# Attention rounds woven into an FFN and expert kernel: normalising written ahead of the transposition, and the weight split of three double rounds written behind their softmax

## The chip, the cores and the metric

One core of a Trainium2 chip runs the whole program in one launch. The metric is the device time of that launch in microseconds (us). Shown for the kernel before are the median of three runs and one execution that was also profiled.

## What is computed

The reference, cut to what matters:

```python
# attention: B 2, H 8, S 768, D 64, n_global 8, n_local 96
scores = q @ k^T / sqrt(D) + bias          # bias: -slope * distance
scores = where(keep, scores, -1e9)         # keep: global keys or a local window
a = exp(scores - max(scores)); a = a / (sum(a) + 1e-9)
x = (a @ v), tokens x 512                  # 1536 tokens
# feed-forward (wff), 512 -> 2048 -> 512
h = x @ w_in; g = h * tanh(softplus(h)); y = g @ w_out
# experts (wts), 4 of 512 -> 1024 -> 512, all tokens through all experts
out = sum over e of p[:, e] * (relu(y @ w1[e]) @ w2[e])
```

All of it is float32. The kernel gets float32 accuracy out of a faster matmul type by splitting each factor into a high part (a cast, `...h`) and a low part (the difference, `...l`), and multiplying high by high, low by high and high by low.

## The kernel before

**Blocks and steps.** The 1536 tokens are three blocks of 512. Block 0 goes through attention and the feed-forward part first (`first_block`, ordered by the string `PLAN`). Then `run` walks over steps `s`: each step is one chunk of hidden columns. Steps 16 to 46 are chunks of the experts for block 0. While they run, the attention of blocks 1 and 2 is woven in: 32 pairs (a tile of 128 queries by two heads), each of which goes through the stages of `Attention`. Then come the feed-forward steps of blocks 1 and 2, and the experts of these two blocks (`late_block`).

**A step with attention.** TensorE does the twelve products of the hidden chunk (`hidden`, line 648), the scores of a pair (lines 265 and 266, tile `s`), the transposition of the pair before (line 205, tile `pt`, four 128x128 pieces, head 0 and head 1 in turn), the twelve products of `project` (line 737, tile `acc`) and the product of the transposed probabilities with the values (line 312, tile `o`).

**The stages of a pair in round r** (`Attention`): `scores(r)`; `softmax(r)`, which first gathers an older output (`of`, lines 329 and 332, `x..h` and `x..l`, lines 333 and 334), then on VectorE adds the bias and finds the row extreme (line 279, tile `t`), and on ScalarE takes the exponential with its row sums (line 290, tile `p`); `norm(r)`, two small VectorE instructions on the row sums (lines 192 and 193, tile `st`) and then the scaling of `p` by two instructions of GpSimd (line 200), or of ScalarE (line 198) for the first three pairs; `trans(r-1)`, the transposition of the pair before and its split (high on ScalarE, line 302; low on VectorE, line 303); `parts`, which splits the q and k of a coming pair (lines 239, 241, 244, 246) and the v of this one (lines 254 and 255); `av(r-2)` with the copies of line 320. A pair is transposed one round after its scores.

**Weights.** `part(s)` splits the weights of a coming step: a high part on ScalarE (`wh`, line 630) and a low part in two instructions on GpSimd (`wl`, line 633). It is called for two steps ahead (`now("part", min(s + 3, last))`).

**Double rounds.** 31 steps don't hold 35 rounds, so steps 27, 35 and 43 (`EXTRA = 11, 19, 27` behind step 16) make two: the first one's scores and softmax stand ahead of `hidden`, its other stages behind it, and the second round follows with the usual places. Below, A is the pair whose softmax is in the first half of such a step, and B the one in its second half; B is transposed in the step behind it (28, 36 and 44).

**What sets the order.** Nothing is rescheduled: each engine executes its instructions in the order in which the Python code issues them, and waits on semaphores where data or a buffer is not ready. The order of the calls in `run` is thus the order on every engine's queue.

Of the kernel before, what the change touches and what calls it, by code (L numbers as in the profile page):

```python
# [543 lines left out]
class Body:  # L544
# [420 lines left out]
    def flush(self):  # L965
        for run in self.later:
            run()
        self.later = []
# [35 lines left out]
    def late_block(self, project):  # L1004
# [22 lines left out]
        for run in held[:2]:  # L1027
            run()
# [9 lines left out]
        for run in held[2:]:  # L1038
            run()
# [170 lines left out]
    def run(self):  # L1210
        tc = self.tc
        ffn = lambda t: [("ffn", t, f) for f in range(NF1)]
        moe = lambda a, b: [("moe", 0, f) for f in range(a, b)]

        cut = NE * NF2 - 1
        steps = ffn(0) + moe(0, cut) + ffn(1) + ffn(2) + moe(cut, NE * NF2)
        last = len(steps)
        self.steps = steps
        self.opens, self.closes = set(), {}
        for s, (kind, t, n) in enumerate(steps):  # L1220
            per = NF1 if kind == "ffn" else NF2
            if n % per == 0 or s == last - 1:
                self.opens.add(s)
            if n % per == per - 1 or n == cut - 1:
                self.closes[s] = 0 if n == NF2 - 1 and kind == "moe" else 1 if s == last - 1 else 2
        self.x, self.y, self.outs, self.nr, self.yf, self.rows = {}, {}, {}, {}, {}, {}
        self.w64, self.w32, self.ws, self.h, self.enr, self.g = {}, {}, {}, {}, {}, {}
        self.seconds = {}
        self.w2, self.wp, self.late, self.held = {}, {}, None, None
        bias = self.bias.rearrange("p h c -> p (h c)")  # L1230
        self.sums, self.rest = [bias[:, 0:1024], bias[:, 1024:2048]], bias[:, 2048:3072]
        ready = dict(fetch=0, narrow=0, part=0)

        def now(what, upto):
            while ready[what] < min(upto, last):
                for _ in getattr(self, what)(ready[what]) or ():
                    pass
                ready[what] += 1

        need = [steps.index(("ffn", t, 0)) for t in range(1, NB)]  # L1240
        ffn_at = lambda s: 0 <= s < last and steps[s][0] == "ffn"
        if self.first:
            att, done = self.first_block(ready, now)
            s0 = NF1
        else:
            att, done, s0 = Attention(self, self.pair, 0), 0, 0
            while att.round():
                pass
            att, self.accumulating = None, True
            self.probabilities()  # L1250
        for s in range(s0, last):
            if s == NF1 and not att:
                att = Attention(self, self.pair, 1, NB - 1)
            if s == need[1]:
                while att and att.round():
                    pass
                att = None
                self.attending.close()
                self.late = self.ctx.enter_context(tc.tile_pool(name="late", bufs=1))
            if self.wide and s < NF1:  # L1260
                while ready["narrow"] < min(s + 3, NF1):
                    now("fetch", ready["narrow"] + 1)
                    now("narrow", ready["narrow"] + 1)
            if ffn_at(s - 1) and done < s:
                self.mish_newton(s - 1)
            if s == NF1 and done < s:

                self.mish_hi(s - 1)
                self.mish_lo(s - 1)
                self.project(s - 2)  # L1270
                self.project(s - 1)
                done = s
            now("part", min(s + 3, last))
            if att:
                att.ahead()
            rest, att = (att, None) if s == need[0] - 2 else (None, att)
            extra = att and s - NF1 in EXTRA
            if extra:
                att.scores()
                att.softmax()  # L1280
            self.hidden(s)
            if extra:
                att.trans()
                att.norm()
                att.parts()
                att.av()
                att.ahead()
            if att:
                att.scores()
            if ffn_at(s):  # L1290
                self.mish_exp(s)
            else:
                self.relu_hi(s)
            if att:
                att.softmax()
            if not ffn_at(s):
                self.relu_lo(s)
            if ffn_at(s - 1) and done < s:
                self.mish_hi(s - 1)
            if ffn_at(s):  # L1300
                self.mish_cap(s)
                self.mish_n(s)
                self.mish_r(s)

                if ffn_at(s - 1):
                    self.mish_lo(s - 1)
            if not self.wide or ready["narrow"] == NF1:
                now("fetch", s + 6)
            follow = bool(s0) and s == NF1 + 1
            if follow:  # L1310
                self.project(done)
                done += 1
            if att and not extra:
                att.trans()
                att.norm()
                att.parts()
            if ffn_at(s - 1) and not ffn_at(s) and done < s:
                self.mish_lo(s - 1)
            if not follow and done <= s - (1 if s0 and att and s < need[0] - 2 else 2):
                self.project(done)  # L1320
                done += 1
            if extra:
                att.trans()
                att.norm()
                att.parts()
            if att and not att.av():
                att = None
            att = att or rest
            for task in {8: (("weights", 0, "in"), ("weights", 1, "in")), 6: (("sums", 0),), 5: (("sums", 1),),
                         3: (("part", 0, "in"), ("weights", 0, "out")), 2: (("part", 0, "sums"),),  # L1330
                         1: (("part", 1, "in"),)}.get(last - s, ()):
                getattr(self, "late_" + task[0])(*task[1:])
        self.late_start()
        self.late_part(0, "out")
        self.late_block(lambda k: self.project(last - 2 + k))
# [61 lines left out]
```

## Time and profile before

| | |
|---|---|
| median of 3 runs | 882.5 us (881.11 to 882.75) |
| the profiled execution | 882.74 us, of it 880.9 us span from the first to the last instruction |
| TensorE busy | 865.2 us, 98% of the span |
| VectorE, ScalarE, GpSimd busy | 575.1, 495.1 and 407.5 us (65%, 56%, 46%) |
| mean granted TensorE clock | 0.997 of full speed |
| chain that ended last | TensorE 80%, VectorE 9%, DMA 4%, issue 2%, ScalarE 2%, GpSimd 1% |

A busy engine is one whose instructions overlap that time; the records of matmuls overlap each other, so a matmul's recorded length is longer than the distance from its start to the next start. A row of the timeline gives start, length, engine, line, tile and operands, and in square brackets the idle time just ahead of the instruction and what ended it by the profile's inference. The attention of blocks 1 and 2 lies between about 141 and 357 us.

### The profile page before, as it was taken

Reading aid. Unit: us, or ns where it says so; the run is one execution under the profiler, and the core shown is the slowest. Engines: PE = TensorE matmul, PEld = TensorE weight load, DVE = VectorE, ACT = ScalarE, POOL = GpSimd, SP = SyncE. Lnnn points to the kernel's source line nnn. Section 1 sums busy time; section 2 is a strip of 40 time slices with the busy share of each in tenths; the row PEclk is TensorE's granted clock in tenths of the full one; section 3 lists DMA queues with packets and bytes.
Section 4 is the critical chain, followed back from the end, with each engine's and each line's share of the span. In section 5 each row is a group of like instructions: output and inputs, shape, how many; then the busy total and the mean of one; then the engine's idle time right before and its main releaser. Section 6 shows DMA issues by size and latency. Waiting matters only on the chain.

```text
span 880.9 us, 11412 instructions
## 1 busy us (share of the span) xinstructions
PE 865.2 (98%) x3892; PEld 677.8 (77%) x3892; DVE 575.1 (65%) x1108; ACT 495.1 (56%) x971; POOL 407.5 (46%) x431
## 2 busy tenths in 40 slices
PE   8899998999999999999999999999999999999997
PEld 4545656888888888888888888788888888888886
DVE  6999996766777775566656667645555555555555
ACT  6667576878877777577675567533333333333330
POOL 4001333777776877555310225554455555544420
PEclk9999999999999999999999999999999999999999
DMA  8479782444444442888555640511111111111002
GB/s 316 171 247 282 263 310 96 162 171 145 168 144 145 167 168 73 307 290 289 223 194 198 241 167 1 186 54 48 48 48 48 49 57 62 49 48 48 1 1 99
DMA packets 40579, 127.47 MB, mean 145 GB/s; under 512 B 4160, under 2 KB 6976, under 8 KB 38464
## 3 DMA queue, kind: packets, MB, share of 16 engines
q1 hardware_dynamic: 39648, 125.32, 40.6%
q0 software_dynamic: 720, 1.31, 0.8%
q8 instruction: 32, 0.52, 0.2%
q14 instruction: 35, 0.29, 0.1%
q10 hardware_dynamic: 144, 0.02, 0.0%
HBM read 97.02 MB, written 28.31 MB: 142 GB/s over the span
## 4 chain that ended last, share of the span: by engine, by line
PE 80%; DVE 9%; DMA 4%; issue 2%; ACT 2%; POOL 1%; SPq 0%; DVEq 0%; ACTq 0%; POOLq 0%
PE acc_l L985 20%; PE acc L737 19%; PE h L648 18%; PE ha L934 9%; PE hx L934 7%; DMA wfirst<-w 2%; PE pt L205 2%; DVE w L612 2%; PE o L312 1%; DVE w L614 1%; DMA qk<-in_qk 1%; DVE w L610 1%; PE acc L821 1%; DVE nr L688 1%; PE s L266 1%
## 5 line engine op out<-in xcount | busy, mean ns | idle before, releaser
L633 POOL TENSOR_TENSOR wl<-w,wh 128x512 fp32r<-128x512 f32 x94 | 123.6, 1335 | 67.5 <-ACT wh L630 54.3
L838 DVE SCALAR_TENSOR_TENSOR big<-acc_l,prob,big 128x512 f32<-128x512 f32 x120 | 88.8, 746 | 78.9 <-PE acc_l L985 78.7
L917 POOL TENSOR_TENSOR zl<-wout,zh 128x512 fp32r<-128x512 f32 x32 | 40.9, 1303 | 85.2 <-ACT zh L915 85.2
L917 POOL TENSOR_TENSOR sumsl<-bias,sumsh 128x512 fp32r<-128x512 f32 x32 | 42.7, 1355 | 69.3 <-ACT sumsh L915 69.3
L947 ACT COPY raw<-ha 128x512 f32<-128x512 f32 x33 | 19.4, 586 | 79.6 <-PE ha L934 79.6
L684 DVE SCALAR_TENSOR_TENSOR nr<-e,n 128x512 f32<-128x512 f32 x48 | 34.1, 711 | 44.1 <-ACT n L679 43.8
L664 ACT ACTIVATE e<-h 128x512 f32<-128x512 f32 x48 | 28.1, 586 | 60.8 <-PE h L648 25.5
L200 POOL TENSOR_SCALAR p<-p,st 128x256 f32<-128x256 f32 (+1 forms) x58 | 41.5, 726 | 36.6 <-ACT v L254 31.9
L648 PE MATMUL h<-y0h,wh 128*128 128x512 f32 x128 | 51.0, 398 | 2.1 <-ACT y0h L754 1.9
L737 PE MATMUL acc<-wh,gh 128*128 128x512 f32 x128 | 52.4, 409 | 0.0
L648 PE MATMUL h<-y0l,wh 128*128 128x512 f32 x128 | 51.0, 398 | 0.7 <-DVE y0l L755 0.7
L648 PE MATMUL h<-y0h,wl 128*128 128x512 f32 x128 | 50.9, 398 | 0.0
L985 PE MATMUL acc_l<-zh,gh 128*128 128x512 f32 x128 | 50.7, 396 | 0.0
L985 PE MATMUL acc_l<-zh,gl 128*128 128x512 f32 x128 | 50.5, 394 | 0.0
L630 ACT CAST wh<-w 128x1024 fp32r<-128x1024 f32 x48 | 50.1, 1045 | 0.7
L985 PE MATMUL acc_l<-zl,gh 128*128 128x512 f32 x128 | 50.4, 394 | 0.0
L737 PE MATMUL acc<-wh,gl 128*128 128x512 f32 x128 | 50.2, 392 | 0.0
L985 PE MATMUL acc_l<-zh,gl_late 128*128 128x512 f32 (+1 forms) x128 | 50.0, 391 | 0.0
L985 PE MATMUL acc_l<-zh,gh_late 128*128 128x512 f32 (+1 forms) x128 | 50.0, 391 | 0.0
L737 PE MATMUL acc<-wl,gh 128*128 128x512 f32 x128 | 50.0, 390 | 0.0
L737 PE MATMUL acc<-gh,wh 128*128 128x512 f32 x128 | 49.8, 389 | 0.0
L737 PE MATMUL acc<-gh,wl 128*128 128x512 f32 x128 | 49.8, 389 | 0.0
(254 smaller groups left out, 2521.3 us busy)
## 6 DMA issues: line engine op xcount, KB each, us to landing
w<-in_wts SPq DMA_DIRECT2D x32, 512.0 KB, 4.6
raw<-in_qkv SPq DMA_DIRECT2D x32, 512.0 KB, 3.6
big<-in_wff SPq DMA_DIRECT2D x10, 1024.0 KB, 6.4
wfirst<-w SPq DMA_DIRECT2D x16, 512.0 KB, 11.0
w<-wfirst SPq DMA_DIRECT2D x16, 512.0 KB, 4.7
wkeep<-wh SPq DMA_DIRECT2D x16, 512.0 KB, 4.0
wkeep<-wl SPq DMA_DIRECT2D x16, 512.0 KB, 3.0
wh<-wkeep SPq DMA_DIRECT2D x16, 512.0 KB, 3.2
```

Of the source, the lines that this page charges most:

```text
L200: nc.gpsimd.tensor_scalar(p, p, r, 0.0, ALU.mult, ALU.add)
L630: (nc.vector.tensor_copy if copy == "vector" else nc.scalar.copy)(hi, w)
L633: getattr(nc, engine or "gpsimd").tensor_tensor(lo[:, c], w[:, c], hi.bitcast(F32)[:, c], ALU.subtract)
L648: nc.tensor.matmul(ps, a[:, c], r[:, kc, :], start=m == 0, stop=m == 3 * KC - 1)
L664: nc.scalar.activation(e, self.h[s], AF.Exp, scale=0.5)
L684: nc.vector.scalar_tensor_tensor(self.nr[s], e, 1.0, n, ALU.add, ALU.mult)
L737: nc.tensor.matmul(acc[:, h], a, r, start=opens and k == 0 and m == 0, stop=closes and k == len(chunks) - 1 and m == 2)
L838: nc.vector.scalar_tensor_tensor(o, acc, p, o, ALU.mult, ALU.add)
L917: nc.gpsimd.tensor_tensor(lo[:, c], w[:, c], hi.bitcast(F32)[:, c], ALU.subtract)
L934: nc.tensor.matmul(ps, a[:, c], r[:, kc, :], start=opens and n == 0, stop=n == 5, skip_group_check=True)
L947: nc.scalar.copy(t[(1, 6, 7).index(m)], ps)
L985: nc.tensor.matmul(o, a[:, c], r[:, w], start=n == 0, stop=n == 5)
```

## The change

Two things, both in the order of calls in `run`. In every round there the call of `norm` is written ahead of `trans` (it was behind). And in the three double steps `part` is no longer called at the start of the step: it is called behind the softmax of the second round and the `relu_lo`.

```diff
-            now("part", min(s + 3, last))
             if att:
                 att.ahead()
             rest, att = (att, None) if s == need[0] - 2 else (None, att)
             extra = att and s - NF1 in EXTRA
-            if extra:
+            if not extra:
+                now("part", min(s + 3, last))
+            else:
                 att.scores()
                 att.softmax()
             self.hidden(s)
             if extra:
+                att.norm()
                 att.trans()
-                att.norm()
                 att.parts()
                 att.av()
                 att.ahead()
...
             if not ffn_at(s):
                 self.relu_lo(s)
+            if extra:
+                now("part", min(s + 3, last))
             if ffn_at(s - 1) and done < s:
                 self.mish_hi(s - 1)
...
             if att and not extra:
+                att.norm()
                 att.trans()
-                att.norm()
                 att.parts()
...
             if extra:
+                att.norm()
                 att.trans()
-                att.norm()
                 att.parts()
```

No computing instruction is added, taken away or resized on any engine; the orders of TensorE and of the DMA queue (SP) stay as they were. Where the other three differ:

GpSimd in the double step 35, before (`x2l` is the low part of a gathered output, `wl` that of the weights, `p_1` is pair A, `p_2` pair B):

```order
L334 TENSOR_TENSOR x2l<-of_2_2903,x2h 128x128
L200 TENSOR_SCALAR p_1_2910<-p_1_2910,st_1_2912 128x256 x2
L255 TENSOR_TENSOR v_1_2949<-raw_122,v_1_2949 128x2x128
L334 TENSOR_TENSOR x2l<-of_3_2967,x2h 128x128
L200 TENSOR_SCALAR p_2_2974<-p_2_2974,st_2_2976 128x256 x2
L255 TENSOR_TENSOR v_2_3016<-raw_123,v_2_3016 128x2x128
```

and in the change:

```order
L334 TENSOR_TENSOR x2l<-of_2_2898,x2h 128x128
L200 TENSOR_SCALAR p_1_2905<-p_1_2905,st_1_2907 128x256 x2
L255 TENSOR_TENSOR v_1_2944<-raw_122,v_1_2944 128x2x128
L334 TENSOR_TENSOR x2l<-of_3_2962,x2h 128x128
L633 TENSOR_TENSOR wl_2979<-w_2669,wh_2978 128x512 x2
L200 TENSOR_SCALAR p_2_2969<-p_2_2969,st_2_2971 128x256 x2
```

The two `wl` instructions stood ahead of the first row before; now they stand directly ahead of the scaling of pair B. Steps 27 and 43 differ in the same way.

ScalarE in the second half of the same step, in the change (`gh` is the high part of the hidden chunk, `p_2` with `st_2` the exponential of pair B, `pt_1` the transposed pair A):

```order
L712 ACTIVATE gh_2960<-h_2912 128x512
L333 CAST x2h<-of_3_2962 128x128
L290 ACTIVATE p_2_2969,st_2_2971<-t_2_2970,st_2_2971 128x256 x2
L630 CAST wh_2978<-w_2669 128x1024
L302 CAST pt_1_3006<-pt_1_3001 128x4x128
L239 CAST qs_0_3009<-raw_122 128x256
```

Before, `L630 wh` stood ahead of the gather of the first half, and `L302` followed `L290` directly.

VectorE in the second half of the same step, before:

```order
L717 SCALAR_TENSOR_TENSOR gl_2981<-h_2917,gh_2965 128x512
L303 TENSOR_TENSOR pt_1_3002<-pt_1_2997,pt_1_3002 128x4x128
L192 TENSOR_SCALAR st_2_2976<-st_2_2976 128x2
L193 RECIPROCAL st_2_2976<-st_2_2976 128x2
L244 TENSOR_TENSOR qs_0_3009<-raw_122,qs_0_3009 64x256
```

and in the change:

```order
L717 SCALAR_TENSOR_TENSOR gl_2976<-h_2912,gh_2960 128x512
L192 TENSOR_SCALAR st_2_2971<-st_2_2971 128x2
L193 RECIPROCAL st_2_2971<-st_2_2971 128x2
L303 TENSOR_TENSOR pt_1_3006<-pt_1_3001,pt_1_3006 128x4x128
L244 TENSOR_TENSOR qs_0_3009<-raw_122,qs_0_3009 64x256
```

The two small instructions on the row sums (`st`) moved ahead of the low part of the transposed pair (`pt`); this is so in every one of the rounds from step 16 on.

## Rows read from the trace of the kernel before

**Rows 1.** The page's busy time by engine, over the whole span:

```profile
PE 865.2 (98%) x3892; PEld 677.8 (77%) x3892; DVE 575.1 (65%) x1108; ACT 495.1 (56%) x971; POOL 407.5 (46%) x431
```

**Rows 2.** The waits of PE: us in total, times, longest:

```profile
PE h L648 <- ACT y0h L754: 1.9, 1, 1.9
...
PE pt L205 <- POOL p L200: 1.1, 3, 0.4
```

**Rows 3.** Busy time by stretch, between two double steps:

```profile
231.00:280.00 49.00, 49.00 (x260) 41.81 (x259) 36.31 (x108) 37.18 (x97) 38.57 (x45) 1.00 0.47 161
```

**Rows 4.** PE in order of time: transpositions in steps 19, 28, 36 and 44:

```profile
167.04 0.27 PE L205 MATMUL pt<-ident,p 128*128 128x128 f32 x1
167.57 0.55 PE L205 MATMUL pt<-ident,p 128*128 128x128 f32 x3 [0.26 <-POOL p L200]
...
230.27 0.55 PE L205 MATMUL pt<-ident,p 128*128 128x128 f32 x3 [0.41 <-POOL p L200]
...
287.53 0.27 PE L205 MATMUL pt<-ident,p 128*128 128x128 f32 x1
288.22 0.55 PE L205 MATMUL pt<-ident,p 128*128 128x128 f32 x3 [0.42 <-POOL p L200]
...
344.37 0.60 PE L205 MATMUL pt<-ident,p 128*128 128x128 f32 x4
```

**Rows 5.** POOL in order of time, step 18, ahead of the first wait:

```profile
165.14 0.46 POOL L334 TENSOR_TENSOR x1l<-of,x1h 128x128 fp32r<-128x128 f32 x1
166.01 1.51 POOL L200 TENSOR_SCALAR p<-p,st 128x256 f32<-128x256 f32 x2 [0.41 <-ACT v L254]
```

**Rows 6.** POOL in order of time, double step 35:

```profile
277.42 2.52 POOL L633 TENSOR_TENSOR wl<-w,wh 128x512 fp32r<-128x512 f32 x2
...
283.76 0.46 POOL L334 TENSOR_TENSOR x2l<-of,x2h 128x128 fp32r<-128x128 f32 x1 [0.52 <-ACT x2h L333]
286.65 1.51 POOL L200 TENSOR_SCALAR p<-p,st 128x256 f32<-128x256 f32 x2 [2.42 <-ACT v L254]
```

**Rows 7.** ACT in order of time, double step 35:

```profile
276.20 1.05 ACT L630 CAST wh<-w 128x1024 fp32r<-128x1024 f32 x1
...
284.82 0.19 ACT L290 ACTIVATION_READ_ACCUMULATOR p<-t,st 128x1 f32 x1
284.91 0.57 ACT L302 CAST pt<-pt 128x512 fp32r<-128x512 f32 x1
```

**Rows 8.** DVE in order of time, double step 35:

```profile
279.88 0.69 DVE L303 TENSOR_TENSOR pt<-pt,pt 128x512 fp32r<-128x512 f32 x1 [1.52 <-ACT pt L302]
280.49 0.16 DVE L192 TENSOR_SCALAR st<-st 128x2 f32<-128x2 f32 x1
...
280.88 0.42 DVE L244 TENSOR_TENSOR qs<-raw,qs 64x256 fp32r<-64x256 f32 x1
281.33 0.85 DVE L246 TENSOR_TENSOR kl<-raw,kh 128x512 fp32r<-128x512 f32 x1
...
286.31 0.17 DVE L193 RECIPROCAL st<-st 128x2 f32<-128x2 f32 x1
```

**Rows 9.** ACT and POOL in the double steps 27 and 43:

```profile
226.97 0.57 ACT L302 CAST pt<-pt 128x512 fp32r<-128x512 f32 x1
...
341.54 0.56 ACT L302 CAST pt<-pt 128x512 fp32r<-128x512 f32 x1
...
343.27 0.93 POOL L200 TENSOR_SCALAR p<-p,st 128x256 f32<-128x256 f32 x2 [2.27 <-DVE st L193]
```

**Rows 10.** DVE and POOL where both split a k at once, and DVE alone:

```profile
142.38 1.48 POOL L246 TENSOR_TENSOR kl<-raw,kh 128x512 fp32r<-128x512 f32 x1
...
142.83 1.58 DVE L246 TENSOR_TENSOR kl<-raw,kh 128x512 fp32r<-128x512 f32 x1
...
154.61 0.69 DVE L246 TENSOR_TENSOR kl<-raw,kh 128x512 fp32r<-128x512 f32 x1
```

**Rows 11.** Busy time by stretch where the clock was lower; PEclk is third from last:

```profile
145.00:149.00 4.00, 3.93 (x10) 3.11 (x11) 1.81 (x4) 0.04 (x1) 1.25 (x2) 0.57 0.71 260
```

## The prediction

> **What bounds the kernel now.** I read the busy time by engine first, then TensorE's waits, then its timeline where a wait is, then the other engines at those places. TensorE is busy 98% of the span [rows 1], and between two double steps it is busy without a gap, 49.00 of 49.00 us, while the other three have over ten us of slack [rows 3]. So in an ordinary round nothing that VectorE, ScalarE or GpSimd do earlier is worth anything, and the change can act only where TensorE waits for the chain that it reorders. TensorE waits for GpSimd's scaling of `p` three times [rows 2]: at transpositions in step 19, and in steps 28 and 36, each just behind a double step [rows 4]. Idle time understates such a loss, since records overlap; I take it from starts. The second piece of a transposition follows the first by 0.09 us where nothing is waited for (four pieces then take 0.35). In step 36 it came 288.22 - 287.53 = 0.69 behind the first, so 0.60 was lost there, and in step 19 0.53 - 0.09 = 0.44. In step 44 there was no wait [rows 4].
>
> **Who releases the scaling.** The page names ScalarE's `v` as releaser of GpSimd's `p`, but `p` doesn't read `v`. The reciprocal of pair B ended at 286.31 + 0.17 = 286.48 and `p` started at 286.65 [rows 6, 8]; in step 43 the same start is put down to the reciprocal [rows 9]. So the true chain is: row sums, `st`, `p`, transposition. The sums were there at 284.82 + 0.19 = 285.01 [rows 7], and `st` waited 1.3 us longer only because it was queued behind the low part of the transposed pair.
>
> **Part 1, normalising ahead.** In every round `st` can now start at the row sums, and takes 280.88 - 280.49 = 0.39 us [rows 8] in the gap in which VectorE sits waiting for ScalarE's copy (1.52 us ahead of `L303` in step 35). So `L303` is not later, and whatever follows on VectorE is up to 0.39 earlier. GpSimd's `p` could start about 1 us earlier. In ordinary rounds TensorE covers that: worth nothing [rows 3]. In the first three pairs it is ScalarE that scales, now ahead of its copy of `pt`; that copy comes later, but the product that needs it stands a whole projection behind. In step 18 the gain is limited by GpSimd's queue: it is busy with `x1l` until 165.14 + 0.46 = 165.60, and `p` started at 166.01 [rows 5], so the transposition of step 19 gains 0.41 (0 to 0.44). One wait is written out that was implied: a transposition reuses the bank of the one before, so it needs that one's `L303`, which `st` no longer guarantees. At the worst place, step 36, `L303` ends near 286.7 by the working below, before the first piece at 287.53.
>
> **Part 2, the weight split behind the second softmax.** Nothing is saved where it stood: ScalarE and GpSimd had idle time there. What counts is what now queues behind it. On ScalarE `wh` (1.05) stands ahead of pair A's copy `L302`, the q, k and v copies and the copies of the output; on GpSimd `wl` (2.52) stands directly ahead of pair B's scaling [rows 6, 7], and B is the pair that TensorE asks for in the next step. In step 35, in the times of the old trace:
> - `L302` started at 284.91 [rows 7]. VectorE's chain into B's exponential is 0.39 earlier, so `wh` starts at 284.52 and ends at 285.57. GpSimd has been idle since `x2l`, ended at 284.22 [rows 6], and starts `wl` some 0.1 later, at 285.67; it ends at 288.19.
> - Then `p`. It took 1.51 us in step 35 and 0.93 in step 43 [rows 6, 9]; the difference is VectorE's split of q and k, which runs over the one and is absent by the other. In the new order `L302` ends near 286.1, `L303` takes 0.61 behind it, and the split 0.45 + 0.85 [rows 8], from 286.7 to 288.0: it lies over `wl` instead, so I take 0.93, and `wl` becomes dearer by what a GpSimd subtraction lost in such an overlap, 1.48 against 2.52 / 2 = 1.26 [rows 6, 10]: 0.2. `p` ends at 289.32, and TensorE goes on 0.06 later (288.16 to 288.22 in rows 4 and 6), at 289.38 in place of 288.22: **+1.2** (+1.0 without the overlap, +1.75 with the slow `p` as well).
>
> I take VectorE's lead as 0.3 in the other two, since there ScalarE's copies of line 320 hold part of it back.
> - Step 27: `L302` at 226.97 [rows 9]; wh from 226.67, `wl` 227.82 to 230.54, `p` to 231.47, TensorE at 231.53 in place of 230.27 [rows 4]: **+1.25** (+1.0 to +1.75).
> - Step 43: `L302` at 341.54 [rows 9]; `wh` to 342.29, `wl` 342.39 to 344.91, `p` (0.93, no q or k to split any more) to 345.84, TensorE at 345.90. It needed that piece at 344.37 + 0.09 = 344.46: **+1.45** (+1.25 to +1.75).
>
> At places like these the Trainium skill has a rule that speaks against the change, in SBUF — State Buffer, Who interferes with whom: a VectorE instruction with two SBUF inputs and a GpSimd instruction that reads SBUF don't share, the one that starts later is blocked for the whole of the other. The trace agrees for most of it: VectorE's split of k took 0.69 alone, 0.85 under `p`, and 1.58 under GpSimd's own split, which itself lost only 0.2 [rows 8, 10]. By the rule in full, a `wl` caught behind both splits would lose 0.42 + 0.69 = 1.1 in place of 0.2, at two of the places.
>
> Other effects I cost at nothing. The weights split later are used in the step after next, with the whole of step 36 between. Their `w` buffer comes free some 8 us later, and the load that takes it is for four steps on. VectorE and ScalarE fall behind by about 1 us in step 36, which is no more than TensorE has lost there. Behind the attention TensorE is bound by its own work, so nothing given away is recovered.
>
> **Sum.** -0.41 + 1.25 + 1.2 + 1.45 = +3.5 us; each place is counted against its own old resume, so they add. Bounds: -0.44 + 1.0 + 1.0 + 1.25 = +2.8, and 0 + 3 x 1.75 = +5.3. The profiled execution took 882.74, which would become 886.2; it stands 0.24 above the median of 882.5, from which I forecast **886.0**.
>
> **Rivals.**
> - *The stalls go (faster).* If the new split were done before TensorE asks for B, the reordered `st` would remove the losses: 0.41 and two of 0.60, and at most VectorE's lead of 0.3 at each of the two, if TensorE also waits there for a bank that VectorE frees: -2.2, 880.3. This needs `wh`, `wl` and `p` to fit between 284.5 and 287.6, 3.1 us, where the rows give 1.05 + 2.52 + 0.93 = 4.5. It decides at a `wl` of some 1.1 us, under half of its row. 6%.
> - *They cancel (no difference).* If the two places that had a wait resume where they did, and only step 43's is new: -0.41 + 1.45 = +1.0, 883.5. For it: the chain would have to be shorter by 1.2 at both, as by softmaxes earlier than I reckon. 12%.
> - *The clock falls.* After its longest wait in the middle of the program, 1.9 us for `y0h` [rows 2], TensorE ran from 145 to 149 us with a granted clock of 0.57 on the mean, mostly at the lower of 1.2 and 2.4 GHz [rows 11], which cost 0.43 x 4.00 = 1.7 us. The new waits are of up to about that size (0.6 + 1.25 in step 28). Against it: the old wait in step 28 left the clock at 1.00 [rows 3, 4], and a transposition breaks each new one in two. One fall makes 887.7, two 889.4. 10%.
> - *Full blocking.* `wl` waits out both of VectorE's splits, 0.42 + 0.69 = 1.1 in place of 0.2 [rows 8, 10], as VectorE lost 0.9 to GpSimd where the two split a k at once: 0.9 more at two places, +5.3, 887.8. 6%. This is the rule of the Trainium skill given above.
>
> **The numbers.** The forecast as such has 66%, with its bounds 885.3 to 887.8. With half of the no-difference case and the single fall of the clock, the range is 884.3 to 888.2. About 0.2% (1.8 us) is what a measurement of this kernel can tell from no change. Slower: 66 + 10 + 6 = 82%; the same 12%; faster 6%.
>
> **What would show it.** Right: in the double steps GpSimd's two `wl` end just ahead of B's `p`; TensorE waits for `p` in steps 28, 36 and 44, at the first piece already, and no longer in step 19; `p` takes about 0.93 there; the clock stays at 1.00. Wrong: no wait in step 44; `p` of pair B starting ahead of 288; a wait in ordinary rounds; or a stretch of lower clock behind one of the three.

## The result and the profile after

The change makes the kernel slower: 889.95 us median of six executions (887.54 to 891.44) against 881.81 (880.78 to 882.75) before, a ratio of 1.009 with a 95% interval of 1.0074 to 1.0105. The forecast of 886.0 had the direction, but its range ended at 888.2. The profiled execution of after took 890.03, of it 888.2 us span; that of before took 882.74, as its table says.

The page of after, busy time by engine:

```profile
PE 867.2 (98%) x3892; PEld 679.2 (76%) x3892; DVE 590.7 (66%) x1108; ACT 495.1 (56%) x971; POOL 400.8 (45%) x431
```

Beside [rows 1] two things moved that no edit explains at first sight: VectorE is busy 15.6 us longer with the same 1108 instructions, and GpSimd 6.7 us less. The waits of PE, after:

```profile
PE pt L205 <- POOL p L200: 5.3, 3, 2.0
...
PE o L312 <- DVE of L332: 0.7, 1, 0.7
```

Three waits for `p` of 1.1 us in all [rows 2] became three of 5.3, and there is a wait for VectorE that was not there. The timeline of PE, after, at the places of [rows 4] and at the new wait in step 35:

```profile
166.80 0.60 PE L205 MATMUL pt<-ident,p 128*128 128x128 f32 x4
...
230.93 1.36 PE L205 MATMUL pt<-ident,p 128*128 128x128 f32 x4 [1.99 <-POOL p L200]
...
286.57 0.71 PE L312 MATMUL o<-pt,v 128*128 128x256 f32 x4 [0.65 <-DVE of L332]
...
292.75 1.00 PE L205 MATMUL pt<-ident,p 128*128 128x128 f32 x4 [1.97 <-POOL p L200]
...
350.92 0.89 PE L205 MATMUL pt<-ident,p 128*128 128x128 f32 x3 [1.37 <-POOL p L200]
```

In step 19 the four pieces run together again (x4 in one row), as before the change they did not. In steps 28, 36 and 44 the first piece waits.

To see what each place cost I pair the n-th matmul of after with the n-th of before (their order is the same) and follow how the distance of their starts grows. From 160 us on it changes at six places: step 19 -0.42; steps 27 and 28 +1.81; between 231 and 235 us, with no wait, +1.44; step 35 +0.55; step 36 +1.90; step 44 +1.93. The sum is +7.2, which is the difference of the profiled executions (7.3). The third of these is no wait at all. Busy time by stretch, after (the number of matmuls stands in brackets behind PE's busy time, PEclk third from last):

```profile
145.00:149.00 4.00, 4.00 (x13) 3.19 (x14) 1.61 (x3) 0.20 (x1) 1.06 (x1) 0.60 0.76 271
231.00:235.00 4.00, 3.90 (x12) 3.10 (x13) 3.60 (x11) 3.00 (x9) 4.00 (x6) 0.57 0.43 140
235.00:284.00 49.00, 49.00 (x260) 41.80 (x260) 38.97 (x103) 34.21 (x90) 31.64 (x43) 1.00 0.42 150
```

Behind the wait of 1.99 us in step 28 the granted clock was 0.57 on the mean, so mostly at the lower of its two levels (1.2 and 2.4 GHz), and TensorE began 12 matmuls in four microseconds, where at the higher clock it begins 260 in 49, so 21 in four. That is +1.44. It is the same sight as [rows 11], which after has too. The last line answers to [rows 3]: between the double steps TensorE is still without a gap.

The spread goes with these falls. The six executions of after fall into pairs by mean granted clock: 887.54 and 888.49 at 0.997, 889.88 and 890.03 at 0.995, 891.05 and 891.44 at 0.993. The profiled one, at 0.995, has two falls (145 us and 231 us), and the profiled one of before, at 0.997, has one. At the same mean clock of 0.997, so with one fall each, after is 5 to 6 us slower (887.54 and 888.49 against executions of before at 882.1 to 882.6); the rest of the 8.1 us between the medians I put down to the clock.

What TensorE waited for in step 36 was made in step 35. Here is that step after the change: ACT in order of time (with the `wh` of steps 27 and 43), then POOL (with the `p` of step 27 and the `wl` and `p` of step 43), then DVE:

```profile
226.16 1.03 ACT L630 CAST wh<-w 128x1024 fp32r<-128x1024 f32 x1
...
286.46 0.30 ACT L333 CAST x2h<-of 128x128 fp32r<-128x128 f32 x1 [1.38 <-DVE of L332]
...
287.98 1.04 ACT L630 CAST wh<-w 128x1024 fp32r<-128x1024 f32 x1
...
346.76 1.03 ACT L630 CAST wh<-w 128x1024 fp32r<-128x1024 f32 x1
```

```profile
229.96 1.37 POOL L200 TENSOR_SCALAR p<-p,st 128x256 f32<-128x256 f32 x2
...
283.97 0.75 POOL L255 TENSOR_TENSOR v<-raw,v 128x256 fp32r<-128x256 f32 x1 [0.17 <-ACT v L254]
286.83 0.46 POOL L334 TENSOR_TENSOR x2l<-of,x2h 128x128 fp32r<-128x128 f32 x1 [2.12 <-ACT x2h L333]
289.10 2.71 POOL L633 TENSOR_TENSOR wl<-w,wh 128x512 fp32r<-128x512 f32 x2 [1.80 <-ACT wh L630]
291.78 1.38 POOL L200 TENSOR_SCALAR p<-p,st 128x256 f32<-128x256 f32 x2
...
347.86 2.54 POOL L633 TENSOR_TENSOR wl<-w,wh 128x512 fp32r<-128x512 f32 x2 [1.79 <-ACT wh L630]
350.38 0.94 POOL L200 TENSOR_SCALAR p<-p,st 128x256 f32<-128x256 f32 x2
```

```profile
284.09 1.17 DVE L246 TENSOR_TENSOR kl<-raw,kh 128x512 fp32r<-128x512 f32 x1
...
288.31 0.17 DVE L193 RECIPROCAL st<-st 128x2 f32<-128x2 f32 x1
...
290.70 1.65 DVE L246 TENSOR_TENSOR kl<-raw,kh 128x512 fp32r<-128x512 f32 x1
```

Read the chain backwards: TensorE (292.75) waits for B's `p` (from 291.78), that stands behind `wl` (from 289.10), and `wl` for `wh` (from 287.98), for which GpSimd stood idle for 1.80 us. The reciprocal that `p` reads was done at 288.48, 3.3 us before `p` began. VectorE's `kl` began at 290.70, under the second `wl` instruction, and ended 0.54 after `wl` did; in that time `p` made little way, and took 1.38 where in step 43, without a `kl`, it took 0.94.

### The profile page after: what moved, and what is told of

The parts are those of the page before. It is cut to its first block, busy times and chain, and to the rows that moved or that the text cites. A ratio compares the mean times of both kernels' runs of the same rounds, so it can differ in the third digit from the quotient of the medians.

```text
span 888.2 us, 11437 instructions
## 1 busy us (share of the span) xinstructions
PE 867.2 (98%) x3892; PEld 679.2 (76%) x3892; DVE 590.7 (66%) x1108; ACT 495.1 (56%) x971; POOL 400.8 (45%) x431
## 4 chain that ended last, share of the span: by engine, by line
PE 79%; DVE 9%; DMA 3%; issue 3%; ACT 2%; POOL 2%; SPq 0%; DVEq 0%; POOLq 0%; ACTq 0%
PE acc_l L985 20%; PE acc L737 18%; PE h L648 18%; PE ha L934 9%; PE hx L934 7%; DMA wfirst<-w 2%; PE pt L205 2%; DVE w L612 1%; PE o L312 1%; DVE w L614 1%; DMA qk<-in_qk 1%; DVE w L610 1%; PE acc L821 1%; DVE nr L688 1%; ACT p L290 1%
## 5 line engine op out<-in xcount | busy, mean ns | idle before, releaser
L630 ACT CAST wh<-w 128x1024 fp32r<-128x1024 f32 x48 | 50.0, 1045 | 0.6
L737 PE MATMUL acc<-gl,wh 128*128 128x512 f32 x128 | 49.8, 389 | 0.0
```

What stands on the lines that cost most here:

```text
L630: (nc.vector.tensor_copy if copy == "vector" else nc.scalar.copy)(hi, w)
L737: nc.tensor.matmul(acc[:, h], a, r, start=opens and k == 0 and m == 0, stop=closes and k == len(chunks) - 1 and m == 2)
```

## Experiments

Three theories were in play. **1:** the loss is GpSimd's queue: the split of the weights stands ahead of B's scaling. **2:** it is norm ahead, whose early `p` runs over VectorE's split of q and k. **3:** it is `wh` on ScalarE, ahead of A's copy and all that follows there.

### Norm ahead alone (e1_norm_only)

The kernel before, with part 1 of the change and without part 2:

```diff
-                att.trans()
                 att.norm()
+                att.trans()
                 att.parts()
```

in all three places.

> The first part of the change alone: norm ahead of trans in every round, the weight split of the double steps at their start as before. Theory 1 (the loss is the queue on GpSimd, the weight split standing ahead of pair B's scaling): no wait in steps 28, 36 and 44, none in step 19; -0.4 - 0.6 - 0.6 = -1.6 us, up to 0.5 given back in step 35 where TensorE now waits for a bank: between -1.9 and -0.9. Theory 2 (the earlier scaling runs over VectorE's split of q and k, and that slowdown is the loss): slower than before by 1 us or more. Theory 3 (the weights' high part standing ahead of pair A's copy on ScalarE is the loss): as theory 1 here. All: the split of k on VectorE takes about 1.17 us in ordinary rounds in place of 0.85.

Measured: 880.86 us median (879.29 to 882.83) against 882.17 of the kernel before on the same chip, ratio 0.9991 (0.9982 to 1.0001). PE in order of time in this kernel, steps 27, 28 and 36:

```profile
225.09 0.47 PE L312 MATMUL o<-pt,v 128*128 128x256 f32 x2 [0.32 <-DVE of L332]
...
229.13 0.60 PE L205 MATMUL pt<-ident,p 128*128 128x128 f32 x4
...
286.25 0.60 PE L205 MATMUL pt<-ident,p 128*128 128x128 f32 x4
```

No wait for `p` is left: step 19 gained 0.43, step 28 0.57, step 36 0.58, and step 35 0.19; step 27 lost 0.42 to a wait for VectorE. Something to be given back was expected, but in step 35. In step 27 it was the `st` of pair A, on VectorE:

```profile
221.07 0.69 DVE L192 TENSOR_SCALAR st<-st 128x2 f32<-128x2 f32 x1 [0.88 <-ACT p L290]
```

Written early, it began while GpSimd was at the step's own `wl`, and took 0.69 in place of 0.16 [rows 8]: it ended at 221.76, `wl` at 221.74. VectorE's split of k took 1.16 on the median, as expected (1.17). So theory 2 can't be the loss of 8 us. The gain is there in the trace; the ratio's interval just includes 1.

### The split moved alone (e2_split_only)

The change, with `norm` behind `trans` again in all three places:

```diff
-                att.norm()
                 att.trans()
+                att.norm()
                 att.parts()
```

> The second part of the change alone: the weight split of the double steps behind the second softmax, norm behind trans as before. Theory 1: waits for the scaling in steps 28, 36 and 44 as long as in the change, +1.5 to +2.0 us each, no gain in step 19: +4.5 to +6.0, and 1.7 more for each fall of the clock. Theory 2: within 1 us of before. Theory 3: as theory 1. VectorE's split of k stays at 0.85 in ordinary rounds.

Measured: 889.91 (889.64 to 890.23), ratio 1.0094 (1.0079 to 1.0109). Places: steps 28 and 36 +1.9 each, step 44 +1.75, and a fall of the clock behind step 36, +1.6. Part 2 alone is the loss. PE, POOL and DVE of this kernel, step 36:

```profile
290.89 0.33 PE L205 MATMUL pt<-ident,p 128*128 128x128 f32 x1 [1.55 <-POOL p L200]
291.77 0.55 PE L205 MATMUL pt<-ident,p 128*128 128x128 f32 x3 [0.55 <-POOL p L200]
```

```profile
287.68 2.52 POOL L633 TENSOR_TENSOR wl<-w,wh 128x512 fp32r<-128x512 f32 x2 [1.80 <-ACT wh L630]
290.18 1.53 POOL L200 TENSOR_SCALAR p<-p,st 128x256 f32<-128x256 f32 x2
```

```profile
289.23 1.25 DVE L244 TENSOR_TENSOR qs<-raw,qs 64x256 fp32r<-64x256 f32 x1
290.51 0.85 DVE L246 TENSOR_TENSOR kl<-raw,kh 128x512 fp32r<-128x512 f32 x1
```

Here VectorE is one instruction later, and it is `qs` that is caught: 1.25 against 0.42 [rows 8]. It ended 0.28 after `wl`. `wl` lost nothing (2.52, as in [rows 6]), and `p`, under which all of `kl` now lies, took 1.53.

### The split behind B's scaling (e3_split_behind_norm)

The change, with one line moved, so that on GpSimd `p` of B goes first and then `wl`; on ScalarE `wh` stays ahead of `L302`:

```diff
-            if extra:
-                now("part", min(s + 3, last))
...
             if extra:
                 att.norm()
+                now("part", min(s + 3, last))
                 att.trans()
```

> As the change, but in the double steps the weight split is written behind the second norm and ahead of trans: GpSimd scales pair B first and splits the weights after it, while on ScalarE the weights' high part still stands ahead of pair A's copy. Theory 1: the three waits vanish, -1.9 to -0.5 us against before. Theory 2: slower by 1 us or more, as in the first run. Theory 3: the waits stay, of 1 us or more each, +3 us or more.

Measured: 881.91 (880.35 to 882.24), ratio 0.9996 (0.9987 to 1.0005). ACT, POOL and PE of this kernel, step 35 and the transposition of step 36:

```profile
284.16 1.04 ACT L630 CAST wh<-w 128x1024 fp32r<-128x1024 f32 x1
```

```profile
284.83 0.93 POOL L200 TENSOR_SCALAR p<-p,st 128x256 f32<-128x256 f32 x2 [1.35 <-DVE st L193]
285.73 2.74 POOL L633 TENSOR_TENSOR wl<-w,wh 128x512 fp32r<-128x512 f32 x2
```

```profile
286.78 0.60 PE L205 MATMUL pt<-ident,p 128*128 128x128 f32 x4
...
290.33 0.71 PE L312 MATMUL o<-pt,v 128*128 128x256 f32 x4 [0.17 <-DVE of L332]
```

`wh` stands behind B's exponential as in the change, `wl` is as dear (2.74), and the loss is gone. This kernel and the change differ in nothing but whether `p` or `wl` goes first on GpSimd, so the order of these three instructions is the cause: theory 1 holds, theory 3 falls as its main part. What the split still costs in its new place is seen in the last row: waits of TensorE for VectorE's `of` in steps 28, 35 and 36, with 0.68, 0.16 and 0.70 us lost around them, about as much as norm ahead wins (0.43, 0.57 and 0.58). Whether that comes from `wh` ahead of `L302` or from `kl`, which took 1.68 under the dearer `wl`, this run doesn't tell.

### Ordinary rounds as before (e4_ordinary_as_before)

The change, with the old order in ordinary rounds only, so that nothing GpSimd does early runs over VectorE's splits in the round ahead of a double step:

```diff
             if att and not extra:
-                att.norm()
                 att.trans()
+                att.norm()
                 att.parts()
```

> As the change, but norm ahead of trans only in the double steps; ordinary rounds in the old order. Theory 1, with the smaller claim that VectorE came late to the double steps because of contention in the ordinary round ahead: three waits, each some 0.3 to 0.5 us shorter than in the change, and none for a bank in step 35; no gain in step 19: +3.5 to +5.0 us, and 1.7 for each fall of the clock. If the lateness is made within the double step: +5 to +6.5, as the change without a fall. Theory 2: within 1 us of before.

Measured: 889.11 (887.97 to 889.84), ratio 1.0085 (1.0071 to 1.0099). Places: steps 27 and 28 +1.8 (+1.81 in the change), a fall of the clock +1.6, steps 35 and 36 together +1.5 (+2.45), step 44 +1.7 (+1.93). Without the fall that is +5.0, on the border of the two ranges expected. The waits of PE for `p` in this kernel, and its POOL and ACT rows of step 35:

```profile
PE pt L205 <- POOL p L200: 5.4, 4, 2.0
```

```profile
290.97 1.36 POOL L200 TENSOR_SCALAR p<-p,st 128x256 f32<-128x256 f32 x2
```

```profile
287.18 1.03 ACT L630 CAST wh<-w 128x1024 fp32r<-128x1024 f32 x1
```

The expectation of shorter waits at all three places was wrong: two stayed as long (1.98 and 1.99), and only that of step 44 was shorter (1.17 in place of 1.37). What went is the wait of step 35 for VectorE: that place cost +0.55 in the change and gained 0.38 here, while step 36 cost 1.9 in both. So the order in ordinary rounds explains about 1 us of the change's loss, nearly all of it at one place. `p` still took 1.36 in step 35, so its stretching is made within the double step.

### The high part cast early (e5_cast_early)

The dose test. GpSimd's order is that of the change, but `wh` is cast at the start of the step, as before the change:

```diff
             else:
+                cut = self.part(ready["part"])
+                next(cut)
+                next(cut)
                 att.scores()
...
             if extra:
-                now("part", min(s + 3, last))
+                for _ in cut:
+                    pass
+                ready["part"] += 1
```

> The change with one thing undone: in the three double steps the high part of the weights (wh) is cast at the step's start again; only the two low parts (wl) stay ahead of pair B's scaling on GpSimd. The same queue order on GpSimd, so a dose of the suspected cause. Theory 1 (the loss is the whole chain wh, wl, p behind B's exponential, run through GpSimd's queue): GpSimd stood idle 1.80, 1.80 and 1.64 us ahead of wl for wh, so wl starts that much earlier and the three waits of TensorE for p (1.99, 1.97, 1.37 in the change) shrink to 0 to 0.4; none is long enough for a fall of the clock; 882.0 to 884.0. Theory 2 (2.5 us of GpSimd work in that place is enough for the loss, wherever wh stands): waits of over 1 us stay, 886 to 890.

Measured: 882.66 (880.98 to 883.11) against 881.18 of the kernel before in this comparison, ratio 1.0008 (0.9999 to 1.0017). POOL in step 35 and PE in step 36:

```profile
282.86 0.46 POOL L334 TENSOR_TENSOR x2l<-of,x2h 128x128 fp32r<-128x128 f32 x1 [2.12 <-ACT x2h L333]
283.28 2.55 POOL L633 TENSOR_TENSOR wl<-w,wh 128x512 fp32r<-128x512 f32 x2
285.81 1.54 POOL L200 TENSOR_SCALAR p<-p,st 128x256 f32<-128x256 f32 x2
```

```profile
286.63 0.27 PE L205 MATMUL pt<-ident,p 128*128 128x128 f32 x1
287.40 0.55 PE L205 MATMUL pt<-ident,p 128*128 128x128 f32 x3 [0.50 <-POOL p L200]
```

`wl` follows `x2l` without the idle 1.80, and TensorE is back where it was before the change, with the stalls of about half a microsecond that it had there. From 160 us on this trace ends 0.2 ahead of before's, that of the change 7.2 behind, of it 1.44 by the clock: 6.0 us went, where GpSimd's idle time for `wh` was 1.80 + 1.80 + 1.79 = 5.4. Theory 2 of this run (2.5 us of GpSimd work in this place is enough) falls: with a `wl` that can start at once TensorE is no later than before. What costs the rest is that `wl` starts only behind a cast that was itself put behind the exponential. But `wl` in this place is not free: norm ahead alone (e1_norm_only) won 0.57 and 0.58 in steps 28 and 36, and here these places stand at +0.08 and +0.09.

### Norm ahead only where it is awaited (e6_ahead_where_awaited)

A version to beat both: the kernel before, with `norm` ahead up to step 19 and in the second half of the double steps:

```diff
             if att and not extra:
+                late = s >= NF1 + 4
+                if not late:
+                    att.norm()
                 att.trans()
-                att.norm()
+                if late:
+                    att.norm()
                 att.parts()
...
             if extra:
-                att.trans()
                 att.norm()
+                att.trans()
                 att.parts()
```

> A try at a version that beats both: the weight split where it was before; norm ahead of trans only in the steps up to 19 and in the second half of the double steps, where TensorE waited for p in the kernel before; in all other rounds the old order, so that GpSimd's scaling doesn't run over VectorE's split of q and k in the rounds ahead of the double steps. Theory (what norm ahead gives, it gives at these places, and elsewhere it only makes VectorE slower): it keeps -0.43 in step 19 and -0.57 and -0.58 in steps 28 and 36, without the +0.42 of step 27: -1.6 to -2.1 in the trace, 880.0 to 880.8, a little better than norm ahead everywhere (880.86). Rival (the +0.42 comes from the double step itself): as norm ahead everywhere, 880.8 to 881.3.

Measured: 880.66 (878.91 to 881.03) against the same 881.18, ratio 0.9983 (0.9974 to 0.9992): the only one of the kernels here that is faster than before by its interval. PE in order of time, steps 19, 27, 28 and 36:

```profile
165.36 0.60 PE L205 MATMUL pt<-ident,p 128*128 128x128 f32 x4
...
223.43 0.47 PE L312 MATMUL o<-pt,v 128*128 128x256 f32 x2
...
227.47 0.60 PE L205 MATMUL pt<-ident,p 128*128 128x128 f32 x4
...
284.79 0.60 PE L205 MATMUL pt<-ident,p 128*128 128x128 f32 x4
```

Steps 19, 28 and 36 gain 0.42, 0.57 and 0.58, and step 27 loses nothing, as the theory says. Its reason for step 27 isn't shown: this kernel has the old order in the first half of the double steps too, so it can't tell the rounds ahead from that half, and the row of 221.07 in e1_norm_only puts the loss of step 27 into that half. From 160 us on it ends 1.7 ahead of before. Its interval overlaps that of e1_norm_only, so which of the two is better the times don't tell.

## Why the prediction was right and wrong

**Right: what bounds the kernel, and the true releaser of `p`.** TensorE was without a gap in ordinary rounds, and nothing was won or lost there. That `p` follows the reciprocal and not ScalarE's `v` is shown by e1_norm_only and e6_ahead_where_awaited, where the reciprocal comes earlier and the waits of steps 28 and 36 go. One reading in it was off: pieces of a transposition that wait for nothing start 0.11 apart (344.37 and 344.48 in step 44), not 0.09. The old losses were thus 0.58 in step 36 and 0.42 in step 19, just what these two runs won there (0.58, and 0.43 and 0.42).

**Right: step 19.** Forecast -0.41, measured -0.42.

**Right in kind: the split behind the second softmax.** `wl` ends just ahead of `p` of B, TensorE waits at the first piece in steps 28, 36 and 44, and the chain is `wh`, `wl`, `p`, as forecast. e3_split_behind_norm and e5_cast_early show it from both ends. `wl` itself, forecast at 2.72, took 2.71.

**Wrong in size: the three terms.** Forecast +1.25, +1.2 and +1.45, measured +1.81 (steps 27 and 28), +2.45 (35 and 36) and +1.93 (44); the sum without the clock is +5.8 in place of +3.5. Two steps of the working failed.

- *"It lies over `wl` instead, so I take 0.93."* `kl` doesn't lie over `wl`: it is held up by it and then lies over `p`. It took 1.65, of which 1.1 under `wl` and 0.54 behind its end, and `p` took 1.37 and 1.38 in steps 27 and 35: +0.44 at each. Only in step 43, which has no `kl`, was it 0.94. The upper bound had a slow `p` ("with the slow `p` as well"), but the centre was at the other end. The rule of the Trainium skill that the prediction had as a rival, in SBUF — State Buffer, Who interferes with whom, says that of two such instructions the later waits for the whole of the other. The traces agree for VectorE as the later one (`qs` 1.25 in place of 0.42 in e2_split_only), and the two `wl` together lost 0.19 at most. The rival had it the wrong way round: it took `wl` for the later one, and for `kl` `wl` was the earlier.
- *"VectorE's chain into B's exponential is 0.39 earlier"*, and 0.3 in the other two. It was not. `wh` began at 226.16, 287.98 and 346.76. `L302` stood at 226.97, 284.91 and 341.54 [rows 7, 9]; with what TensorE had shifted ahead of the step (-0.70, +2.55, +5.02, on the two traces' own time) that is 226.27, 287.46 and 346.56. So in place of 0.3, 0.39 and 0.3 early `wh` was 0.11 early, 0.52 late and 0.20 late, which adds 0.2, 0.9 and 0.5. The 0.52 of step 35 is the new wait for `of`. In e4_ordinary_as_before, with the old order in ordinary rounds, `wh` of step 35 began at 287.18; the old place shifted there is 284.91 + 2.71 = 287.62. So there the lead was real, 0.44, and it is norm ahead in ordinary rounds that undid it. I had taken "whatever follows on VectorE is up to 0.39 earlier" as free, and given it a lower end of zero; that it could come out as a loss was not in the bounds.

With these, 1.25 + 0.44 + 0.2 = 1.9, 1.2 + 0.44 + 0.9 = 2.5 and 1.45 + 0.5 = 1.95, against 1.81, 2.45 and 1.93 measured.

**Wrong: "norm ahead" costs VectorE nothing.** Before, GpSimd's `p` began while VectorE was already splitting q and k. With `st` early, `p` and `v` begin first, and the splits run into them. The groups of the trace by line (line, count, then busy us and mean ns), before and then after:

```profile
L200 POOL TENSOR_SCALAR p<-p,st 128x256 f32<-128x256 f32 (+1 forms) x58 | 41.5, 726 | 36.6 <-ACT v L254 31.9 <-DVE st L193 2.9 <-ACT kh L241 1.7
...
L246 DVE TENSOR_TENSOR kl<-raw,kh 128x512 fp32r<-128x512 f32 x30 | 25.6, 854 | 1.1
...
L192 DVE TENSOR_SCALAR st<-st 128x2 f32<-128x2 f32 x32 | 6.5, 203 | 0.0
```

```profile
L246 DVE TENSOR_TENSOR kl<-raw,kh 128x512 fp32r<-128x512 f32 x30 | 32.5, 1084 | 1.0
...
L200 POOL TENSOR_SCALAR p<-p,st 128x256 f32<-128x256 f32 (+1 forms) x58 | 28.9, 511 | 16.4 <-ACT pt L302 13.1 <-ACT qs L239 2.4 <-DVE st L193 0.8
...
L192 DVE TENSOR_SCALAR st<-st 128x2 f32<-128x2 f32 x32 | 10.9, 341 | 9.9 <-ACT p L290 9.9
```

GpSimd's scaling became 12.6 us cheaper, VectorE's `kl` 6.9 and its `st` 4.4 dearer: the overlap changed sides. This is the 15.6 us of the page, most of it. It hurts only where TensorE then waits for VectorE, directly or through `wh`: with the old order in ordinary rounds (e4_ordinary_as_before) steps 35 and 36 lost about 1 us less, and step 44 0.2 less.

**Too low: the fall of the clock, at 10%.** I had set against it that the old wait of step 28 left the clock at 1.00, and that a transposition breaks each new wait in two. But in the change the first piece took the whole wait, 1.99, which is the size of the one ahead of [rows 11]. Behind step 28 or 36 the clock fell once in each profile of a kernel that waited there for 1.55 to 1.99 us at a time (the change, e2_split_only, e4_ordinary_as_before), and in none of the others; behind the waits of 1.17 to 1.37 us in step 44 it didn't. That the waits bring the falls is read from this alone; no run changes the wait and nothing else. By their mean clock the executions of the change had one to three falls in all, that at 145 us among them.

**The other rivals.** That the stalls go would have needed `wh`, `wl` and `p` within 3.1 us; in step 35 they took 5.2, from 287.98 to 293.16. Full blocking of `wl` by VectorE did not come: 2.71. What the range lacked was a case with both an unfavourable chain and a clock that falls.

## What to carry to other kernels

An instruction that nothing needs for a long time, put ahead of one that the bounding engine awaits, costs the whole wait for its own input as well as its run: here 2.5 us of work used up the 0.6 us that norm ahead wins at a place when they could start at once, but made each of the three transpositions 1.8 to 1.9 us later than in the kernel before when GpSimd first stood idle 1.8 us for a cast. When a reorder lets one of VectorE and GpSimd start earlier, cost the instruction of the other that it will now run over, and ask of each pair which comes first, since it is the later one that pays. And a forecast that makes a busy TensorE wait 2 us should carry the chance of a fall of its clock in its range together with the dearest chain, not as a rival apart.

## What was not expected of the hardware

- The same `kl` on VectorE took 0.69 where GpSimd was idle as it began [rows 10], 0.85 under GpSimd's `p` [rows 8], 1.17 where it began under `v` (rows of 284.09 and 283.97 above), and 1.65 under `wl`. In the last two it ended 0.54 behind the GpSimd instruction.
- A VectorE instruction of two elements a partition can be held up as well. After, in step 28, VectorE and then the GpSimd row that it ran under:

```profile
233.38 1.17 DVE L192 TENSOR_SCALAR st<-st 128x2 f32<-128x2 f32 x1 [0.28 <-ACT p L290]
```

```profile
231.99 2.54 POOL L633 TENSOR_TENSOR wl<-w,wh 128x512 fp32r<-128x512 f32 x2
```

The `st` instruction takes 0.16 alone [rows 8]; here it ended at 234.55, as `wl` did at 234.53.
- After waits of 2 us the clock fell at one place and not at another (in the profile of the change behind step 28, at 1.99, and not behind step 36, at 1.97); each fall cost 1.4 to 1.6 us. A kernel's times come in steps: the executions of the kernel before lie at 880.7 to 881.2 (mean clock mostly 0.999) and at 882.1 to 882.8 (mostly 0.997), but for one at 883.9. The profiled one, at 0.997, has its fall at 145 us; that of e6_ahead_where_awaited, at 1.00, has the same wait for `y0h` of 1.9 us and no fall there.
